# A GpSimd mask split in two and moved, and a fourth buffer for `u`, in a fused linear-attention and MLP kernel

## The chip, the cores and the metric

The kernel runs on one core of a Trainium2 chip. The metric is the device time of one execution in microseconds, lower is better. The profile is one execution, taken apart by the hardware profiler. Its engines are called PE (TensorE, with its weight loads as PEld), DVE (VectorE), ACT (ScalarE), POOL (GpSimd) and SP (SyncE).

## The reference

Sequence 2048, width 640, 32 heads of 20, MLP width 1728, bfloat16 inputs.

```
def A(x, wqkv, w_phi, wo):                       # linear attention
    q, k, v = (x @ wqkv) split into 3 x 32 heads of 20
    pq, pk = q @ w_phi[h], k @ w_phi[h]
    phi_q = concat(softmax(pq), softmax(-pq));  phi_k the same from pk
    kv, z = sum over s of phi_k[s] v[s]^T, sum over s of phi_k[s]
    o = (phi_q @ kv) / (phi_q @ z + 1e-6)
    return o @ wo

h   = x + A(layernorm(x), wqkv, w_phi, wo)
out = h + silu(layernorm(h) @ w1) @ w2
```

The state `kv` is 20 x 20 numbers for each head and sign, summed over the whole sequence, so no output of the attention can begin before the last key and value.

## The kernel before

The 2048 tokens lie on 128 partitions in 16 tiles of 640 columns. The whole program is a list of words, `ORDER`, written out by hand: each word names a small function `op_..`, with its tile or chunk, an engine or queue, and the PSUM banks (behind `@`). Every engine runs its own instructions in the order of that list; semaphores, found from the data, hold an instruction until what it reads is written and until the buffer it writes is free. So an instruction that waits holds back all that stands behind it on its engine, and nothing else.

The phases, which overlap:

1. *Statistics and weights.* `st.t` makes mean and variance of tile t on VectorE. `rs.a.b` makes 1/sqrt of the variance of tiles a to b-1, on GpSimd by a power (L275), with the negative mean beside it (L277 or L282 and L283); for a single tile the small constant is added on VectorE (L272), else on GpSimd (L274). `xn.t` normalises (L291 on VectorE, L296 on ScalarE). It is transposed by TensorE and copied out (`xt.t` at L302, `xc.t`), or by a DMA of SP's (`xd.t`). The key weights are folded with `w_phi` beforehand: `wt`, `wc` transpose them (L316, L166), `fk.c` multiplies (L331) and `fc.c` casts chunk c to `Wfk` on ScalarE (L168).
2. *Keys and values.* `kp.t` and `vp.t` are the projections (L364), 2 halves of 5 chunks each; `ke`, `kr`, `kn` make the softmax, the last one mostly on GpSimd (L407); `cc.t` adds to the state in PSUM (L420).
3. *The state's layout.* `mt` transposes a mask, and `km` multiplies the state with it into `KVBD`, which is block diagonal. The mask is `maskR`, [128, 5, 3, 32]: GpSimd sets it to one and clears it with two selects for the even and two for the odd of its five blocks (`op_mc`, L207 to L215). `mt` reads it (L221); nothing else does.
4. *Queries.* `qp`, `qe` project and exponentiate; `dp.t` multiplies by `KVBD` into four PSUM banks (L486); `dw.t` scales and adds the two signs on VectorE into `u` [128, 4, 8, 21] in float32 in SBUF (reciprocal L500, L501, then L507 and L510); `dr.t` takes the reciprocal of the denominator (L515); `do.t.half` writes a half of the output `o` on GpSimd or VectorE (L521), and is the last reader of `u`.
5. *Output projection and MLP.* `td.t` transposes `o` by a DMA, `op.t` projects (L548), `oa.t` adds the residual (L557), `sq`, `sr`, `hn`, `hd` normalise again, `up` and `ua` are the first MLP layer and SiLU (L627, L637, L649), `yp`, `yh` the second (L673, L686), `yo` adds and stores.

At the change the list reads, in words of GpSimd alone: `rs.0.1`, `mc`, `rs.1.2`, `rs.2.3`, `rs.8.10`, `rs.3.4`, `rs.10.12`. The tiles go through `dw` in the order 0, 1, 3, 2, 4, 6, 5, 9, 7, 8, 13, 12, 11, 15, 10, 14, and `u` has three buffers; a `u` takes whichever buffer is read out first. The pool that holds `u` is opened only after the state is closed, in the place of the first phases' tiles.

Of the kernel before, what the change touches and what calls it, by code (L numbers as in the profile page):

```python
# [9 lines left out]
ALU = mybir.AluOpType  # L10
# [8 lines left out]
F32 = mybir.dt.float32  # L19
# [5 lines left out]
ORDER = """  # L25
lx.0.1.a lk.0.1.s lp.a lx.1.2.s lk.4.5.a lk.1.2.s lk.2.3.s lk.3.4.s mk mo wm.512@7 wm.512@7 wm.512@7
wm.512@7 wm.512@7 wm.512@7 wm.512@7 wm.512@7 wm.512@7 wm.256@7 wt.0@0 st.0 rs.0.1 wm.256@2 wm.128@2 wt.4@1
ph ta mc st.1 wc.0.a wt.1@2 lx.2.4.s wc.1.v fk.0@4 wt.2@3 wc.2.v lx.8.12.s wc.4.a fc.0.a fk.4@6 fc.4.a
rs.1.2 xn.0.v fk.1@0 fc.1.a wt.3@2 wc.3.v fk.2@4 fc.2.a xt.0@3 xn.1.v xc.0.v st.2 rs.2.3 st.9 fk.3@6 fc.3.a
xn.2.v xt.1@2 st.8 xc.1.a rs.8.10 kp.0@0 ke.0 kp.1@4 lv.0.3.s ke.1 lv.3.5.s xt.2@3 xc.2.a vp.1@6 lq.1.s st.3  # L30
rs.3.4 st.10 vc.1.a xn.3.v xn.8.a vp.0@0 vc.0.a vp.2@4 vc.2.a xt.3@2 xc.3.a xn.9.v st.11 rs.10.12 xn.11.a
lx.4.8.s kp.2@6 st.7 ke.2 vp.3@0 lx.12.16.s kp.3@4 ke.3 xd.9 kp.9@2 st.6 xd.8 vp.8@6 xn.10.v rs.6.8 vc.3.a
xd.10 xn.6.a lq.4.s st.4 st.5 rs.4.6 xn.4.a ke.9 xn.5.a kr.0 kr.1 kn.0.p vp.9@4 vc.9.a kp.8@0 kn.1.p xd.11
vc.8.a st.13 xn.7.a kr.9 kn.9.p kp.10@2 ke.10 st.12 rs.12.14 kr.3 kn.3.p ke.8 vp.10@4 vc.10.a xd.6 kr.8
kn.8.p vp.6@6 vc.6.a kr.2 lq.3.s xn.13.a vp.11@2 vc.11.a xd.4 vp.4@0 vc.4.a kp.4@4 lq.2.s gk.2@6 st.15 xd.5
gk.1@2 kp.5@0 st.14 xd.7 ke.4 kr.4 gc.2.a xn.12.a kp.6@4 cc.3 gc.1.a ke.5 cc.0 ke.6 cc.8 cc.9 rs.14.16
xn.14.a mt kr.5 cc.1 kn.2.q lq.0.s xd.13 kp.13@2 ke.13 kr.13 l1.0.s l1.1.s vp.5@0 vc.5.a xn.15.v kr.10 xd.12
kn.5.p kn.13.q vp.13@4 vc.13.a xd.14 kp.12@2 ke.12 kr.12 kn.10.p kp.11@0 ke.11 kr.6 vp.7@4 vc.7.a gk.4@2
vp.12@0 kn.4.q l2.0.2.s l2.2.4.s gc.4.a gk.3@4 gc.3.a kp.14@2 vp.14@4 vc.14.a kn.12.p cc.2 cc.5 kr.11 ke.14
# [28 lines left out]
def kernel(  # L68
# [11 lines left out]
    nc = tc.nc  # L80

    P = nc.NUM_PARTITIONS
    T = 16
    D = 640
    C = 5
    H = 32
    DH = 20
# [11 lines left out]
    H0 = [(32 * r) // DH for r in range(C)]  # L99
# [48 lines left out]
    maskR = first.tile([P, C, 3, 32], BF16, name="maskR")  # L148
# [23 lines left out]
    def wk2():  # L172
        return late["work"]
# [29 lines left out]
        for vp in Vps:  # L203
            nc.gpsimd.memset(vp[:, :, DH : DH + 1], 1.0)

    def op_mc():
        nc.gpsimd.memset(maskR[:], 1.0)  # L207
        for r0 in range(2):
            m = maskR[:, r0::2, :, :]
            n, b0 = (C + 1 - r0) // 2, 32 * r0 - DH * H0[r0]  # L210
            nc.gpsimd.affine_select(
                out=m, in_=m, compare_op=ALU.is_ge, fill=0.0,
                base=b0, pattern=[[64 - 3 * DH, n], [-DH, 3], [1, 32]], channel_multiplier=0,
            )
            nc.gpsimd.affine_select(  # L215
                out=m, in_=m, compare_op=ALU.is_gt, fill=0.0,
                base=DH - b0, pattern=[[3 * DH - 64, n], [DH, 3], [-1, 32]], channel_multiplier=0,
            )

    def op_mt():  # L220
        nc.vector.transpose(  # L221
# [274 lines left out]
    def op_dw(t, how="p"):  # L496
        A = tl["dp", t]
        first = A[0][:, :, :, 0:21]
        w = sm.tile([P, 4, 8], F32, name="w")
        nc.vector.reciprocal(w[:], A[1][:, :, :, 21])  # L500
        nc.vector.tensor_tensor(w[:], w[:], A[0][:, :, :, 21], op=ALU.mult)  # L501
        if how == "c":
            kept = wk2().tile([P, 4, 8, 21], F32, name="kept", bufs=1)
            nc.scalar.copy(kept[:], first)
            first = kept[:]
        u = wk2().tile([P, 4, 8, 21], F32, name="u", bufs=3)
        nc.vector.tensor_tensor(  # L507
            u[:], A[1][:, :, :, 0:21], w[:].unsqueeze(3).to_broadcast([P, 4, 8, 21]), op=ALU.mult,
        )
        nc.vector.tensor_tensor(u[:], u[:], first, op=ALU.add)  # L510
        tl["u", t] = u[:].rearrange("p (a k) h c -> p a (k h) c", a=2)
# [228 lines left out]
```

## Time and profile before

| | |
|---|---|
| three runs | 239.09, 239.43, 240.14 us; median 239.43 |
| the profiled execution | 238.86 us, of which the span of the trace is 237.2 |
| granted TensorE clock | 1.00 |
| TensorE busy | 229.9 us, 97% |
| VectorE, ScalarE, GpSimd busy | 133.7, 114.9 and 92.9 us |
| DMA, mean over the span | 87 GB/s |

A row of the timeline or of a group has the start and the duration in us (the groups a mean in ns), engine, line and operation, the tiles written and read, shapes and count, and in brackets the idle time of the engine ahead of it with what ended it. Ends of matmuls are modelled, and rows that follow each other closely may overlap by some hundredths of a us. The chain of waits follows the last instruction back, at each step to what released it.

### The profile page before, as it was taken

What the parts mean: (1) busy time and instruction counts of PE and PEld (TensorE: products, weight loads), DVE (VectorE), ACT (ScalarE), POOL (GpSimd) and SP (SyncE); (2) the same over time, 40 slices, a digit from 0 to 9 for tenths busy, and PEclk for the clock granted to TensorE, in tenths of its full rate; (3) what the DMA queues carried; (4) which work ended last, traced back from release to release, by engine and by line L of the source; (5) the groups of instructions that cost most, each with busy time, mean ns of one, the idle gap of its engine ahead of it and who ended that gap; (6) DMA issues with size and microseconds to landing.
All of it is one profiled execution on the core that took longest, in us unless ns stands there. A gap on an engine that the chain in (4) does not pass through costs nothing.

```text
span 237.2 us, 6320 instructions
## 1 busy us (share of the span) xinstructions
PE 229.9 (97%) x2672; PEld 147.6 (62%) x2672; DVE 133.7 (56%) x257; ACT 114.9 (48%) x172; POOL 92.9 (39%) x184
## 2 busy tenths in 40 slices
PE   6899999999999999999999999999999999999995
PEld 2677777777544555886754645556654657688762
DVE  3899999899838989988878504321203000220032
ACT  3788998866866575664054254654014240013000
POOL 7656897798923454188071600534000100000000
PEclk9999999999999999999999999999999999999999
DMA  7964768495001849123734411103211100020012
GB/s 209 305 239 92 128 118 184 120 249 175 3 6 31 179 80 197 37 53 62 113 83 86 83 30 28 29 12 75 72 41 55 28 28 3 28 83 3 0 60 83
DMA packets 44845, 20.68 MB, mean 87 GB/s; under 512 B 34448, under 2 KB 44304, under 8 KB 44816
## 3 DMA queue, kind: packets, MB, share of 16 engines
q1 hardware_dynamic: 43728, 19.88, 36.1%
q10 hardware_dynamic: 1088, 0.39, 0.7%
q8 instruction: 21, 0.34, 0.6%
q14 instruction: 8, 0.07, 0.1%
HBM read 9.61 MB, written 2.62 MB: 52 GB/s over the span
## 4 chain that ended last, share of the span: by engine, by line
PE 88%; DVE 4%; POOL 4%; ACT 1%; DMA 1%; issue 1%; DVEq 0%; POOLq 0%
PE mm L673 24%; PE mm L627 23%; PE mm L364 18%; PE mm L548 8%; PE mm L451 7%; PE mm L486 3%; PE mm L420 2%; ACT EqT L461 1%; DMA X<-in_A_x_dram 1%; PE mm L686 1%; DVE u L507 1%; DVE u L510 1%; PE mm L637 1%; POOL RS L275 1%; PE mm L331 1%
## 5 line engine op out<-in xcount | busy, mean ns | idle before, releaser
L627 PE MATMUL mm<-HnT,w 128*128 128x512 bf16 (+1 forms) x325 | 59.1, 337 | 0.0
L649 ACT ACTIVATE shT<-mm 128x1024 bf16<-128x1024 f32 (+2 forms) x29 | 27.7, 963 | 64.3 <-PE mm L627 48.8
L673 PE MATMUL mm<-w,shT 128*128 128x320 bf16 (+2 forms) x416 | 58.5, 299 | 0.0
L673 PEld LDWEIGHTS <-shT 128*128 128x128 bf16 x416 | 39.7, 98 | 17.7 <-issue 0.8
L627 PEld LDWEIGHTS <-w 128*128 128x128 bf16 x325 | 31.3, 98 | 22.8 <-issue 0.3
L694 DVE TENSOR_TENSOR ob<-mm,X 128x640 bf16<-128x640 f32 x15 | 12.0, 817 | 47.0 <-PE mm L673 29.3
L364 PEld LDWEIGHTS <-XnT 128*128 128x128 bf16 x320 | 30.7, 98 | 11.8 <-issue 0.2
L407 POOL TENSOR_TENSOR Ek<-Ek,Sk 128x1280 bf16<-128x1280 bf16 (+2 forms) x16 | 34.6, 2184 | 3.1 <-DVE Sk L400 2.2
L557 DVE SCALAR_TENSOR_TENSOR X<-mm,X 128x640 bf16<-128x640 f32 x16 | 13.1, 823 | 21.5 <-PE mm L548 21.3
L397 DVE TENSOR_REDUCE Sk<-Ek 128x64 f32<-128x1280 bf16 x16 | 23.3, 1456 | 1.6 <-ACT Ek L389 1.6
L548 PE MATMUL mm<-wo,ot 128*128 128x320 bf16 x160 | 23.9, 299 | 0.2 <-ACT EqT L461 0.2
L521 POOL TENSOR_TENSOR o<-u,rd 128x320 bf16<-128x320 f32 x20 | 14.7, 752 | 22.7 <-DVE rd L515 14.4
L364 PE MATMUL mm<-Wfk,XnT 128*128 128x320 bf16 x160 | 23.4, 299 | 0.0
L451 PE MATMUL mm<-XnT,Wfq 128*128 128x512 bf16 x100 | 23.3, 380 | 0.0
L461 ACT ACTIVATE EqT<-mm 128x1024 bf16<-128x1024 f32 (+1 forms) x24 | 19.6, 884 | 7.4 <-PE mm L451 7.4
L364 PE MATMUL mm<-wv,XnT 128*128 128x320 bf16 x160 | 23.2, 299 | 0.0
L389 ACT ACTIVATE Ek<-mm 128x640 bf16<-128x640 f32 x32 | 20.6, 710 | 3.2 <-PE mm L364 2.7
L548 PEld LDWEIGHTS <-ot 128*128 128x128 bf16 x160 | 15.4, 98 | 7.4 <-issue 0.7
L565 ACT ACTIVATE sq<-X 128x640 bf16<-128x640 bf16 x16 | 11.7, 730 | 9.3 <-DVE X L557 7.7
L267 DVE BATCH_NORM_STATS2 stats<-X 128x6 f32<-128x320 bf16 x32 | 13.7, 468 | 3.8 <-DMA X<-in_A_x_dram 3.8
L577 POOL TENSOR_SCALAR hm<-hst,hm 128x1 f32<-128x1 f32 x16 | 4.6, 290 | 28.0 <-ACT sq L565 27.0
L451 PEld LDWEIGHTS <-Wfq 128*128 128x128 bf16 x100 | 9.1, 98 | 9.9
(78 smaller groups left out, 214.0 us busy)
## 6 DMA issues: line engine op xcount, KB each, us to landing
out_dram<-ob SPq DMA_DIRECT2D x15, 160.0 KB, 1.8
w<-in_B_w_dram SPq DMA_DIRECT2D x6, 360.0 KB, 5.2
X<-in_A_x_dram SPq DMA_DIRECT2D x3, 640.0 KB, 6.6
w<-in_B_w_dram SPq DMA_DIRECT2D x5, 320.0 KB, 4.9
wk<-in_A_wqkv_dram SPq DMA_DIRECT2D x4, 160.0 KB, 4.2
wv<-in_A_wqkv_dram SPq DMA_DIRECT2D x1, 480.0 KB, 7.3
wo<-in_A_wo_dram SPq DMA_DIRECT2D x1, 480.0 KB
w<-in_B_w_dram SPq DMA_DIRECT2D x1, 480.0 KB, 4.0
```

Source lines behind the costliest of these rows:

```text
L267: nc.vector.bn_stats(stats[:, k, :], X[:, t, k * 320 : (k + 1) * 320])
L364: nc.tensor.matmul(ps[:, half, 0:320], tok(XnT[t // GT], t)[:, c, :], W[:, c, half * 320 : (half + 1) * 320], start=(c == 0), stop=(c == C ...
L389: nc.scalar.activation(Ek[:, s, :].rearrange("p (a n) -> p a n", a=2), tl["kp", t][:, :, 0:320], AF.Exp, scale=1.0 - 2.0 * s,)
L397: nc.vector.tensor_reduce(Sk[:], tl["ek", t][:].rearrange("p s (h f) -> p (s h) f", f=DH), axis=AX.X, op=ALU.add,)
L407: nc.gpsimd.tensor_tensor(Ek3[:, 0:n], Ek3[:, 0:n], Sk[:, 0:n].unsqueeze(2).to_broadcast([P, n, DH]), op=ALU.mult,)
L451: nc.tensor.matmul(ps[:, k, :], Wfq[:, c, r * P : (r + 1) * P], XnT[g][:, c, :], start=(c == 0), stop=(c == C - 1),)
L461: nc.scalar.activation(E[:, s, rs[0] : rs[-1] + 1, :], tl["qp", g, i][:, 0 : len(rs), :], AF.Exp, scale=1.0 - 2.0 * s,)
L521: (nc.vector if eng == "v" else nc.gpsimd).tensor_tensor(tl["o", t][:, a * 320 : (a + 1) * 320].rearrange("p (h f) -> p h f", f=DH), tl["u ...
L548: nc.tensor.matmul(ps[:, half, 0:320], tl["ot", t][:, c, :], wo[:, c, half * 320 : (half + 1) * 320], start=(c == 0), stop=(c == C - 1),)
L627: nc.tensor.matmul(ps[:, i * W : (i + 1) * W], w1[:, c, fc * P : (fc + 1) * P], HnT[g][:, c, 0:W], start=(c == 0), stop=(c == C - 1), skip ...
L649: nc.scalar.activation(sh[:, a:b], tl["up", g, k][:, 0 : b - a], AF.Silu)
L673: nc.tensor.matmul(ps, shT[g][:, fc * W + i * P : fc * W + (i + 1) * P], w2[:, fc, a:b], start=first and fc == 0, stop=last and fc == FC - ...
```

## The change

`op_mc` takes an argument. `mc.0` sets the whole mask to one and does the two selects of the even blocks; `mc.1` does the two of the odd ones. `mc.0` now stands behind `rs.2.3` and `mc.1` behind `rs.3.4`, so GpSimd's order is `rs.0.1`, `rs.1.2`, `rs.2.3`, `mc.0`, `rs.8.10`, `rs.3.4`, `mc.1`, `rs.10.12`. The same five instructions are issued. The tile `u` gets four buffers for three. No other instruction changes place on any engine; in the built program the only waits that differ besides are those for a buffer of `u`, and one of an `hn` that had been covered by such a wait.

```
 ORDER
-ph ta mc st.1 wc.0.a ...
+ph ta st.1 wc.0.a ...
-... xc.0.v st.2 rs.2.3 st.9 fk.3@6 fc.3.a
+... xc.0.v st.2 rs.2.3 mc.0 st.9 fk.3@6 fc.3.a
-... st.3 rs.3.4 st.10 vc.1.a ...
+... st.3 rs.3.4 mc.1 st.10 vc.1.a ...

-    def op_mc():
-        nc.gpsimd.memset(maskR[:], 1.0)
-        for r0 in range(2):
-            m = maskR[:, r0::2, :, :]
+    def op_mc(r0):
+        if r0 == 0:
+            nc.gpsimd.memset(maskR[:], 1.0)
+        m = maskR[:, r0::2, :, :]
             (the two selects as before)

-        u = wk2().tile([P, 4, 8, 21], F32, name="u", bufs=3)
+        u = wk2().tile([P, 4, 8, 21], F32, name="u", bufs=4)
```

More of the change, by code (lines that the diff above doesn't have):

```diff
@@ L27 @@
 wm.512@7 wm.512@7 wm.512@7 wm.512@7 wm.512@7 wm.512@7 wm.256@7 wt.0@0 st.0 rs.0.1 wm.256@2 wm.128@2 wt.4@1
-ph ta mc st.1 wc.0.a wt.1@2 lx.2.4.s wc.1.v fk.0@4 wt.2@3 wc.2.v lx.8.12.s wc.4.a fc.0.a fk.4@6 fc.4.a
-rs.1.2 xn.0.v fk.1@0 fc.1.a wt.3@2 wc.3.v fk.2@4 fc.2.a xt.0@3 xn.1.v xc.0.v st.2 rs.2.3 st.9 fk.3@6 fc.3.a
+ph ta st.1 wc.0.a wt.1@2 lx.2.4.s wc.1.v fk.0@4 wt.2@3 wc.2.v lx.8.12.s wc.4.a fc.0.a fk.4@6 fc.4.a rs.1.2
+xn.0.v fk.1@0 fc.1.a wt.3@2 wc.3.v fk.2@4 fc.2.a xt.0@3 xn.1.v xc.0.v st.2 rs.2.3 mc.0 st.9 fk.3@6 fc.3.a
 xn.2.v xt.1@2 st.8 xc.1.a rs.8.10 kp.0@0 ke.0 kp.1@4 lv.0.3.s ke.1 lv.3.5.s xt.2@3 xc.2.a vp.1@6 lq.1.s st.3
[L31 to L36, printed above, removed]
+rs.3.4 mc.1 st.10 vc.1.a xn.3.v xn.8.a vp.0@0 vc.0.a vp.2@4 vc.2.a xt.3@2 xc.3.a xn.9.v st.11 rs.10.12
+xn.11.a lx.4.8.s kp.2@6 st.7 ke.2 vp.3@0 lx.12.16.s kp.3@4 ke.3 xd.9 kp.9@2 st.6 xd.8 vp.8@6 xn.10.v rs.6.8
+vc.3.a xd.10 xn.6.a lq.4.s st.4 st.5 rs.4.6 xn.4.a ke.9 xn.5.a kr.0 kr.1 kn.0.p vp.9@4 vc.9.a kp.8@0 kn.1.p
+xd.11 vc.8.a st.13 xn.7.a kr.9 kn.9.p kp.10@2 ke.10 st.12 rs.12.14 kr.3 kn.3.p ke.8 vp.10@4 vc.10.a xd.6
+kr.8 kn.8.p vp.6@6 vc.6.a kr.2 lq.3.s xn.13.a vp.11@2 vc.11.a xd.4 vp.4@0 vc.4.a kp.4@4 lq.2.s gk.2@6 st.15
+xd.5 gk.1@2 kp.5@0 st.14 xd.7 ke.4 kr.4 gc.2.a xn.12.a kp.6@4 cc.3 gc.1.a ke.5 cc.0 ke.6 cc.8 cc.9 rs.14.16
 xn.14.a mt kr.5 cc.1 kn.2.q lq.0.s xd.13 kp.13@2 ke.13 kr.13 l1.0.s l1.1.s vp.5@0 vc.5.a xn.15.v kr.10 xd.12
@@ L204, in op_mo @@
             nc.gpsimd.memset(vp[:, :, DH : DH + 1], 1.0)
-    def op_mc():
-        nc.gpsimd.memset(maskR[:], 1.0)
-        for r0 in range(2):
-            m = maskR[:, r0::2, :, :]
[L210 to L218, printed above, removed]
+    def op_mc(r0):
+        if r0 == 0:
+            nc.gpsimd.memset(maskR[:], 1.0)
+        m = maskR[:, r0::2, :, :]
+        n, b0 = (C + 1 - r0) // 2, 32 * r0 - DH * H0[r0]
+        nc.gpsimd.affine_select(
+            out=m, in_=m, compare_op=ALU.is_ge, fill=0.0,
+            base=b0, pattern=[[64 - 3 * DH, n], [-DH, 3], [1, 32]], channel_multiplier=0,
+        )
+        nc.gpsimd.affine_select(
+            out=m, in_=m, compare_op=ALU.is_gt, fill=0.0,
+            base=DH - b0, pattern=[[3 * DH - 64, n], [DH, 3], [-1, 32]], channel_multiplier=0,
+        )
     def op_mt():
```

## The prediction

> **What bounds the kernel now.** I read the page's busy table first, then the busy time by stretches, cut at the two places where the chain of waits leaves TensorE for long.
>
> ```profile
> span 237.2 us, 6320 instructions
> PE 229.9 (97%) x2672; PEld 147.6 (62%) x2672; DVE 133.7 (56%) x257; ACT 114.9 (48%) x172; POOL 92.9 (39%) x184
> ```
>
> ```profile
> 10.25:69.73 59.48, 59.48 (x953) 41.68 (x954) 53.24 (x93) 48.07 (x78) 44.70 (x46) 1.00 0.60 137
> 69.73:125.15 55.42, 53.82 (x842) 33.78 (x840) 48.38 (x102) 30.06 (x45) 25.86 (x64) 1.00 0.46 92
> 125.15:234.40 109.25, 109.20 (x807) 67.45 (x806) 26.22 (x49) 31.08 (x43) 13.93 (x43) 1.00 0.17 42
> ```
>
> The rows of the stretches give the stretch, its length, then busy time of PE, PEld, DVE, ACT, POOL, the granted clock, and DMA. TensorE works 59.48 of 59.48 us in the first of them and 109.20 of 109.25 in the last, at clock 1.00. So no edit to another engine gains anything inside those two, and a gain made ahead of one of them is carried to the end unless some wait inside it lacks slack. In the stretch between, TensorE is idle for 1.60 us, in exchanges with VectorE and ScalarE that start from TensorE's own work and so move with it. What can be won is idle time of TensorE: 237.2 less 229.9, 7.3 us, 2.8 of it behind its last matmul at 234.40. The list of waits says who waited for whom (total, times, longest), and the timeline has the wait at the head of the first full stretch.
>
> ```profile
> PE mm L486 <- DVE u L510: 1.4, 4, 0.5
> DVE u L507 <- POOL o L521: 1.3, 1, 1.3
> ```
>
> ```profile
> 10.25 0.45 PE L302 MATMUL mm<-ident,xn 128*128 128x128 bf16 x5 [0.61 <-DVE xn L291]
> ```
>
> Two waits lie under the change: the 0.61 us before the transposes of tile 1 (L302), which waited for `xn`, and one of the four waits of L486 for `u`. The row between them is VectorE's own wait for a `u` buffer, once, 1.3 us. The chain shows why `xn` came late:
>
> ```profile
> 6.78 0.44 POOL maskR L207
> ...
> 9.20 0.52 POOL RS L275
> 9.72 0.03 issue
> 9.75 0.46 DVE xn L291
> ```
>
> The mask is built from 6.78 to 9.20 us, in front of the power of `rs.1.2` (tile 1), for which `xn.1` and then TensorE wait.
>
> **The mask, first gain.** What `mc` leaves behind, on VectorE, TensorE and ScalarE (start, duration):
>
> ```profile
> 8.02 0.14 DVE L272 TENSOR_SCALAR RS<-MV 128x1 f32<-128x1 f32 x1
> 8.08 0.44 DVE L291 TENSOR_SCALAR xn<-X,MV,RS 128x640 bf16<-128x640 bf16 x1
> 8.60 0.49 DVE L166 COPY wTk<-mm 128x640 bf16<-128x640 bf16 x1
> 9.75 0.45 DVE L291 TENSOR_SCALAR xn<-X,MV,RS 128x640 bf16<-128x640 bf16 x1 [0.66 <-POOL RS L275]
> 10.11 0.48 DVE L166 COPY XnT<-mm 128x640 bf16<-128x640 bf16 x1
> 9.15 0.49 PE L331 MATMUL mm<-phb,wTk 128*128 128x140 bf16 x6
> 10.65 2.89 PE L364 MATMUL mm<-Wfk,XnT 128*128 128x320 bf16 x20
> 7.33 3.16 ACT L168 CAST Wfk<-mm 128x640 bf16<-128x640 f32 x5
> ```
>
> With the mask gone, GpSimd is free when VectorE's variance of tile 1 is done, at 8.02 + 0.14 = 8.16. The power takes 0.52, so it is there at about 8.8, and VectorE is busy with the copy of `wTk` until 9.09. Hence `xn.1` starts at 9.09 and VectorE's whole idle 0.66 us goes. The copy to `XnT` that follows (`xc.0`) ends at 10.59 now and at 9.93 then. TensorE's `kp.0` starts at 10.65, 0.06 behind that copy, and could start at 9.99; the transposes in between (`xt.1`) no longer wait, since `fk.3` ends at 9.64.
>
> What is late next: the key projection adds five chunks, and chunk 3 needs the fourth row block of `Wfk`, which ScalarE casts last of five. That row ends at 7.33 + 3.16 = 10.49 and does not move, because the casts run back to back. A matmul of that row takes 2.89 / 20, about 0.14, so chunk 3 would be due at 9.99 + 0.41 = 10.40 and can start at about 10.54; now it starts at 10.65 + 0.41 = 11.06. **The first gain is 0.52 us**, between 0 (should a further wait stand at the same place) and 0.66 (should the cast not hold it).
>
> **Where the mask goes.** `mc.0` is a memset and two selects behind `rs.2.3`, `mc.1` two selects behind `rs.3.4`. GpSimd's rows there:
>
> ```profile
> 6.71 0.50 POOL L207 MEMSET maskR<- 128x480 bf16 x1
> 8.28 0.47 POOL L211 TENSOR_SCALAR_AFFINE_SELECT maskR<-maskR 128x192 bf16<-128x192 bf16 x1
> 8.82 0.38 POOL L215 TENSOR_SCALAR_AFFINE_SELECT maskR<-maskR 128x192 bf16<-128x192 bf16 x1
> 9.17 0.54 POOL L275 TENSOR_TENSOR RS<-RS,nhalf 128x1 f32<-128x1 f32 x1
> 14.29 0.24 POOL L274 TENSOR_SCALAR RS<-MV 128x2 f32<-128x2 f32 x1 [1.47 <-DVE MV L268]
> 18.36 0.22 POOL L274 TENSOR_SCALAR RS<-MV 128x2 f32<-128x2 f32 x1 [1.43 <-DVE MV L268]
> ```
>
> From start to start `mc.0` costs 8.28 - 6.71 = 1.57 us and `mc.1` 9.17 - 8.28 = 0.89. The pauses are 1.47 and 1.43. VectorE's stream runs 0.66 ahead, so both pauses move and keep their lengths; `mc.0` overruns its own by 0.10. Queued behind it are `rs.8.10`, then the power of `rs.3.4`, for which VectorE's `xn.3` waits, and behind that TensorE's `xt.3`:
>
> ```profile
> 16.44 0.80 DVE L291 TENSOR_SCALAR xn<-X,MV,RS 128x640 bf16<-128x640 bf16 x2
> 17.73 0.44 PE L302 MATMUL mm<-ident,xn 128*128 128x128 bf16 x5
> ```
>
> Those `xn` come 0.66 - 0.10 = 0.56 earlier, TensorE only 0.52, and 17.73 - 17.24 = 0.49 us of slack lie between them already. So the mask costs nothing in its new places; without that cover it would cost the 0.10. `mc.1` has 0.54 to spare, and its reader, the transpose of the mask, comes near 40 us. No DMA is moved past anything.
>
> **The fourth `u`, second gain.** The late rows:
>
> ```profile
> 103.69 0.73 POOL L521 TENSOR_TENSOR o<-u,rd 128x320 bf16<-128x320 f32 x1
> 109.69 0.86 DVE L507 TENSOR_TENSOR u<-mm,w 128x672 f32<-128x672 f32 x1
> 110.84 1.54 POOL L521 TENSOR_TENSOR o<-u,rd 128x320 bf16<-128x320 f32 x2
> 121.90 0.19 DVE L501 TENSOR_TENSOR w<-w,mm 128x32 f32<-128x32 f32 x1
> 122.59 0.73 POOL L521 TENSOR_TENSOR o<-u,rd 128x320 bf16<-128x320 f32 x1
> 123.35 0.86 DVE L507 TENSOR_TENSOR u<-mm,w 128x672 f32<-128x672 f32 x1 [1.27 <-POOL o L521]
> 124.24 0.85 DVE L510 TENSOR_TENSOR u<-u,mm 128x672 f32<-128x672 f32 x1
> 123.89 0.74 PE L637 MATMUL mm<-HnT,w 128*64 128x256 bf16 x10
> 125.15 0.46 PE L486 MATMUL mm<-KVBD,EqT 32*128 32x44 bf16 x40 [0.52 <-DVE u L510]
> ```
>
> At 123.35 `u` of tile 15 takes the buffer that tile 12 leaves, and GpSimd reads that one last at 122.59 to 123.32. With four, the built program lets it take the buffer of tile 7, read out in the row at 110.84. It then starts at about 122.1, 1.27 us earlier, and the PSUM banks that TensorE's L486 (`dp.10`) waits for are free at 123.8 in place of 125.09. TensorE's matmul before it ends at 124.63, so the wait of 0.52 goes whole, and what is late next is TensorE itself. A follower starts about 0.05 before the modelled end of the one ahead (10.25 + 0.45 against 10.65), so **the second gain is 0.52 to 0.57; I take 0.57**. The rest of VectorE's 1.27 buys nothing, for the stretch behind has 0.05 us of idle on TensorE. The one new wait, of tile 12's `u` at 109.69 on GpSimd's row at 103.69, was over 5 us before. The other waits for `u` that go, or move to an earlier reader, cost nothing now: the list has one such wait. The other three waits of L486 are the plain sequence of matmul, two `u` steps and matmul on the same banks, and stay.
>
> **The sum.** 0.52 + 0.57 = 1.09 us off the span of 237.2. The profiled run took 238.86, 1.66 us around its span, and would take 237.8. The median of the three runs is 239.43, 0.57 above it; carried over, 1.1 us give **238.3**, 0.46% less. A measurement of this kernel can tell about 0.5%, 1.2 us, from no change.
>
> **Rivals.** *One gain only.* A wait with little slack takes one of the two back. Against it: the two full stretches, and the 0.49 us at `xt.3`, the tightest place under the mask. It gives 239.43 - 0.52, 238.9. Chance 0.10.
>
> *Nothing happens.* The mask or the buffer was put down to the wrong wait; both rows name the releaser, and the built order shows the moves, so 0.05, at 239.4.
>
> *Slower: `mc.0` stretches in its new place.* It would run beside VectorE's statistics and `xn.2`. For `xt.3` to cost TensorE anything, `mc.0` must take over the 0.49 of slack and the 0.60 by which it would let `rs.8.10` start early; each us beyond is lost. With the second gain kept, the kernel is slower by 1.2 us when `mc.0` takes 1.09 + 0.57 + 1.2 = 2.9 us more than its 1.57, nearly three times as long; at three times (3.1 more) the kernel would take about 240.9. The rows at 8.28 and 8.82 speak against it: the first ran beside the `xn` at 8.08 and took 0.47, the second has the same shape and took 0.38, so a collision costs some 0.09, and one for each of the three instructions, 0.27, stays inside the 0.49. The Trainium skill, "GPSIMD Engine Reference", Key points, has the rule that speaks against this change: GpSimd shares its SBUF interfaces with VectorE and contends with VectorE's instructions in a two-port mode or with two SBUF inputs; it gives no figure, and by it the sum could lie anywhere down to this rival's. The trace agrees in sign, with that 0.09 us. Chance 0.07.
>
> **How the numbers follow.** Both gains arrive with 0.78, one with 0.10, none with 0.05, the slower case with 0.07. In the first case the gain lies between 0.52 + 0.52 = 1.04 and 0.66 + 0.57 = 1.23 by the bounds, and three runs of one kernel spread over 239.09 to 240.14, so 1.2 us is nearly a coin's toss. What was counted at nothing (VectorE 1.27 us ahead behind 122, fewer semaphore waits) can only add, so I give that side a little more: 0.48 over 0.5%, 0.30 within. Within gets the next two cases as well, 0.45. The range runs from the upper bound (238.2) less the 0.34 by which the lowest run lies below the median, with 0.15 for what was counted at nothing, 237.7, to the one-gain case plus about as much, 239.2.
>
> **What would show it.** In the new trace TensorE's wait at L302 for `xn` is gone, `kp.0` starts near 10.0 with a short stop inside it before 10.54, GpSimd's mask rows begin near 14.29 - 1.47 - 0.66 = 12.2 and 18.36 - 1.43 - 0.66 = 16.3, TensorE's second stretch is still full, and L486 near 124.0 has no wait while VectorE's for GpSimd's `o` is gone. Wrong it would be if `mc.0` took well over 1.6 us, if `xt.3` waited, or if TensorE showed a new wait behind 126 us.

## The result, and the profile after

The changed kernel takes 238.37 us (median of 10 runs, 237.92 to 238.61), beside 239.08 for the kernel before on the same chip (10 runs): a ratio of 0.9964, 95% interval 0.9951 to 0.9976. (The ratios are not the quotients of the medians, which lie 0.71 us or 0.30% apart here.) By the ratio that is 0.36% less, inside the 0.5% that was set as the bound of what a measurement tells from no change, though the interval lies wholly below 1. The forecast was 238.3 and 0.46% less. The profiled execution's span is 236.4 us, 0.8 less than before, at a granted clock of 1.00.

The page's busy table, and the busy time by stretches, cut at the same matmuls as before (stretch, length, then PE, PEld, DVE, ACT, POOL, clock, DMA share, GB/s):

```profile
span 236.4 us, 6319 instructions
PE 230.5 (97%) x2672; PEld 147.5 (62%) x2672; DVE 134.1 (57%) x257; ACT 115.1 (49%) x172; POOL 93.0 (39%) x184
```

```profile
9.34:69.29 59.95, 59.93 (x956) 41.62 (x954) 53.35 (x93) 48.77 (x79) 47.14 (x51) 1.00 0.61 141
124.12:233.38 109.26, 109.20 (x809) 67.44 (x807) 25.71 (x48) 31.56 (x43) 13.66 (x43) 1.00 0.18 43
```

TensorE is as full as it was, in both. But the first stretch is 59.95 us long for the same work that took 59.48: it got 0.47 longer, and since ends of matmuls are modelled, the row calls the difference busy. Only the starts of the matmuls tell where it went. The waits (total, times, longest) and TensorE's timeline at the head:

```profile
PE mm L486 <- DVE u L510: 0.8, 3, 0.4
```

```profile
8.99 0.49 PE L331 MATMUL mm<-phb,wTk 128*128 128x140 bf16 x6
9.34 0.45 PE L302 MATMUL mm<-ident,xn 128*128 128x128 bf16 x5
9.74 2.98 PE L364 MATMUL mm<-Wfk,XnT 128*128 128x320 bf16 x20
12.72 0.45 PE L302 MATMUL mm<-ident,xn 128*128 128x128 bf16 x5
13.01 4.28 PE L364 MATMUL mm<-wv,XnT 128*128 128x320 bf16 x30
17.13 0.44 PE L302 MATMUL mm<-ident,xn 128*128 128x128 bf16 x5
```

L486 waits three times for `u`, no longer four. At 9.34 `xt.1` has no bracket any more. `kp.0` lasts 2.98 for 2.89 and `vp` 4.28 where other runs show 4.24: inside them are short stops.

VectorE, ScalarE and GpSimd there, then the late place on VectorE and TensorE:

```profile
8.44 0.49 DVE L166 COPY wTk<-mm 128x640 bf16<-128x640 bf16 x1
8.85 0.44 DVE L291 TENSOR_SCALAR xn<-X,MV,RS 128x640 bf16<-128x640 bf16 x1
11.22 0.89 DVE L267 BATCH_NORM_STATS2 stats<-X 128x6 f32<-128x320 bf16 x2 [0.32 <-DMA X<-in_A_x_dram]
12.27 0.39 DVE L291 TENSOR_SCALAR xn<-X,MV,RS 128x640 bf16<-128x640 bf16 x1
6.97 3.24 ACT L168 CAST Wfk<-mm 128x640 bf16<-128x640 f32 x5
```

```profile
8.11 0.67 POOL L275 TENSOR_TENSOR RS<-RS,nhalf 128x1 f32<-128x1 f32 x1 [1.17 <-DVE RS L272]
11.84 0.50 POOL L208 MEMSET maskR<- 128x480 bf16 x1
12.41 0.60 POOL L211 TENSOR_SCALAR_AFFINE_SELECT maskR<-maskR 128x288 bf16<-128x288 bf16 x1
13.08 0.49 POOL L215 TENSOR_SCALAR_AFFINE_SELECT maskR<-maskR 128x288 bf16<-128x288 bf16 x1
13.80 0.24 POOL L274 TENSOR_SCALAR RS<-MV 128x2 f32<-128x2 f32 x1 [0.23 <-DVE MV L268]
16.39 0.61 POOL L211 TENSOR_SCALAR_AFFINE_SELECT maskR<-maskR 128x192 bf16<-128x192 bf16 x1
17.07 0.38 POOL L215 TENSOR_SCALAR_AFFINE_SELECT maskR<-maskR 128x192 bf16<-128x192 bf16 x1
17.87 0.23 POOL L274 TENSOR_SCALAR RS<-MV 128x2 f32<-128x2 f32 x1 [0.42 <-DVE MV L268]
```

```profile
121.75 0.86 DVE L507 TENSOR_TENSOR u<-mm,w 128x672 f32<-128x672 f32 x1
122.64 0.85 DVE L510 TENSOR_TENSOR u<-u,mm 128x672 f32<-128x672 f32 x1
123.45 0.74 PE L637 MATMUL mm<-HnT,w 128*64 128x256 bf16 x10
124.12 0.47 PE L486 MATMUL mm<-KVBD,EqT 32*128 32x44 bf16 x40
```

GpSimd's power of tile 1 follows VectorE's variance, `xn.1` follows the copy of `wTk`, the two parts of the mask stand in pauses that still end in a wait for VectorE (0.23 and 0.42 us), and `u` of tile 15 and `dp.10` have no wait.

Start by start against before, TensorE stands as follows:

```
at (after)   shift    change  what
  7.63       -0.18            the first weights landed earlier: not the edit's doing
  9.34       -0.91    -0.73   xt.1 without its wait
 10.26       -0.81    +0.10   chunk 3 of kp.0 behind ScalarE's last cast
 12.72       -0.65    +0.16   xt.2 behind xn.2, which stood behind a statistic whose x landed late
 13.47       -0.60    +0.06   values behind the second part of wv, landed at 13.42
 43.10       -0.44    +0.18   a stop for which the profile names no releaser
124.12       -1.03    -0.59   dp.10 without its wait
233.33       -1.03            TensorE's end; the last stores end 0.3 later behind it, so the span gains 0.8
```

Without the 0.18 that the earlier landing of the weights gave, TensorE's end gained 0.85 in this profile.

### The profile page after: what moved, and what is told of

Same layout as the page of the kernel before. It is cut to its first block, busy times and chain, and to the rows that moved or that the text cites. A ratio compares the mean times of both kernels' runs of the same rounds, so it can differ in the third digit from the quotient of the medians.

```text
span 236.4 us, 6319 instructions
## 1 busy us (share of the span) xinstructions
PE 230.5 (97%) x2672; PEld 147.5 (62%) x2672; DVE 134.1 (57%) x257; ACT 115.1 (49%) x172; POOL 93.0 (39%) x184
## 4 chain that ended last, share of the span: by engine, by line
PE 92%; DVE 2%; DMA 2%; ACT 1%; issue 0%; ACTq 0%; DVEq 0%
PE mm L627 24%; PE mm L673 24%; PE mm L364 19%; PE mm L548 9%; PE mm L451 7%; PE mm L486 3%; PE mm L420 2%; DMA wk<-in_A_wqkv_dram 2%; PE mm L331 2%; ACT EqT L461 1%; PE mm L637 1%; PE mm L686 1%; DVE u L507 1%; DVE u L510 1%; PE mm L302 1%; PE mm L316 1%
## 5 line engine op out<-in xcount | busy, mean ns | idle before, releaser
L565 ACT ACTIVATE sq<-X 128x640 bf16<-128x640 bf16 x16 | 11.7, 731 | 9.3 <-DVE X L557 7.7
```

## The experiments

Each was run beside the kernel before on the same chip; ratios are to that kernel, times are medians. The kernel before measured 239.25 beside the first four, 239.21 beside the next six, and 239.16 beside the last two.

**The changed kernel again.**

> The changed kernel as it is, beside its parts on the same chip. Theory of the prediction (two waits of TensorE removed, carried to the end): 0.7 to 1.1 us less than the kernel before; TensorE's last matmul ends about 1.0 us earlier, 0.4 to 0.6 of it won before 70 us and 0.59 at 124 us. Rival (landings of the first loads and stops of TensorE without a wait decide, and differ from run to run): the shift before 70 us differs from the first profile's -0.44 by 0.2 or more, while the 0.59 stays.

238.09 us, ratio 0.9958 (0.9944 to 0.9971): 1.16 us less, a little over the range that was expected. TensorE ends 1.04 ahead of the kernel before, 0.45 of it won before 70 us and 0.59 at 124, as the theory had it.

**The mask alone.**

```
-        u = wk2().tile([P, 4, 8, 21], F32, name="u", bufs=4)
+        u = wk2().tile([P, 4, 8, 21], F32, name="u", bufs=3)
```

> The mask moved in two parts, u with three buffers. Theory: the first gain alone, TensorE ahead by 0.4 to 0.6 us from 20 us to 120 us, the 1.27 us wait of VectorE for GpSimd's o and TensorE's 0.52 us at L486 near 124 us are there again, the time 0.4 to 0.6 us under the kernel before. Rival (the gain in front is taken back later, and only the buffer counts): no difference from before at the end, though the transposes of tile 1 start early.

238.67 us, 0.9977 (0.9966 to 0.9987): 0.58 less. The waits for `u` are back:

```profile
DVE u L507 <- POOL o L521: 1.2, 1, 1.2
PE mm L486 <- DVE u L510: 1.3, 4, 0.5
```

The median is as expected, the profile is not: TensorE ends only 0.15 ahead of the kernel before. The key weights landed late in it, and TensorE's first matmul on them started at 6.71 for 6.24. Counted from there, the gain is 0.62.

**The fourth `u` alone.**

```
+ph ta mc st.1 wc.0.a ...        (the mask in its old place, in one piece)
-... rs.2.3 mc.0 st.9 ...
+... rs.2.3 st.9 ...
-... rs.3.4 mc.1 st.10 ...
+... rs.3.4 st.10 ...
```

> The fourth u alone, the mask as before. Theory: TensorE unchanged up to 124 us with its 0.61 us wait at L302 near 10 us, then 0.59 us ahead to the end, so 0.5 to 0.6 us under the kernel before; with the mask alone this adds up to the whole change within 0.3. Rival (the wait for u hides another, which then takes its place): under 0.2 us won, with a new wait of TensorE behind 125 us.

238.82 us, 0.9984 (0.9974 to 0.9994): 0.43 less. TensorE's timeline has the early wait, not the late one, and near 43 us a stop that the kernel before did not have:

```profile
10.40 0.45 PE L302 MATMUL mm<-ident,xn 128*128 128x128 bf16 x5 [0.61 <-DVE xn L291]
44.10 1.53 PE L364 MATMUL mm<-wv,XnT 128*128 128x320 bf16 x10 [0.28 <-issue]
125.22 0.47 PE L486 MATMUL mm<-KVBD,EqT 32*128 32x44 bf16 x40
```

So in this profile, where the key weights also came 0.16 later than before, TensorE ends 0.08 behind the kernel before, although `dp.10` gained its 0.59; the 0.43 is the median of twelve runs, a little under what was expected.

The two parts give 0.58 + 0.43 = 1.01 us, both together 1.16: within the intervals they add up, and each is worth about half, as the sum had it.

**The whole mask in one pause.**

```
-... rs.2.3 mc.0 st.9 ...      -... rs.3.4 mc.1 st.10 ...
+... rs.2.3 mc.0 mc.1 st.9 ...  +... rs.3.4 st.10 ...
```

> Both parts of the mask behind rs.2.3, in the first pause; four u. Theory: the mask then takes about 2.5 us where the pause has 1.5 to 1.7, so rs.8.10 and rs.3.4 come about 0.7 to 0.9 us later than in the changed kernel; the transposes of tile 3 had 0.6 us of slack there, so TensorE loses 0.1 to 0.3 us and the time lies 0.1 to 0.3 above the changed kernel. Rival (the second pause is not needed, some other cover hides it all): no difference from the changed kernel, and no wait of TensorE at L302 near 17 us. Other rival (GpSimd's selects run much slower there): more than 0.6 us lost.

238.39 us, 0.9969 (0.9959 to 0.9979): 0.30 more than the changed kernel beside it, with intervals that overlap. The timeline of GpSimd and VectorE:

```profile
14.26 0.24 POOL L274 TENSOR_SCALAR RS<-MV 128x2 f32<-128x2 f32 x1
16.41 0.80 DVE L291 TENSOR_SCALAR xn<-X,MV,RS 128x640 bf16<-128x640 bf16 x2 [0.70 <-POOL RS L275]
```

The mask now takes the pause whole (2.40 us, from 11.78), and VectorE waits 0.70 us for the power behind it. TensorE's `xt.3` loses only 0.03: the slack there swallows the rest. But start by start against the changed kernel, TensorE stops 0.09 at 18.64, 0.11 at 35.69 and 0.11 at 39.23, places that the expectation did not name and for which the profile names no releaser. Whether the later mask is behind them is not shown.

**A first part three times as long.**

```
-        nc.gpsimd.affine_select(...)              (the two selects)
+        for _ in range(4 if r0 == 0 else 1):
+            nc.gpsimd.affine_select(...)          (the two selects)
```

> The changed kernel with the two selects of mc.0 done four times instead of once (the same mask comes out), so that mc.0 takes 6 x 0.5 = about 3.0 to 3.3 us more. Theory of the prediction (a cover of about 0.5 us at the transposes of tile 3, beyond which each us is lost): rs.8.10 and rs.3.4 come 2.8 to 3.2 us later than in the changed kernel, of which some 0.3 is the rest of the pause; TensorE waits for xn at L302 near 17 to 19 us and the time lies 2.0 to 2.7 us above the changed kernel, 1.0 to 1.7 above the kernel before. Rival (GpSimd's mask has much more cover than counted, so the slower case could never have come): under 0.7 us above the changed kernel.

241.16 us, 1.0099 (1.0066 to 1.0133): 1.95 more than before. GpSimd, VectorE and TensorE (this kernel's line numbers are one higher):

```profile
17.25 0.24 POOL L275 TENSOR_SCALAR RS<-MV 128x2 f32<-128x2 f32 x1
19.39 0.80 DVE L292 TENSOR_SCALAR xn<-X,MV,RS 128x640 bf16<-128x640 bf16 x2 [3.19 <-POOL RS L276]
19.90 0.45 PE L303 MATMUL mm<-ident,xn 128*128 128x128 bf16 x5 [2.31 <-DVE xn L292]
```

From start to start `mc.0` takes 5.06 us here, 3.49 over the 1.57 of the forecast. `xt.3` starts 2.77 later than in the changed kernel, and TensorE was 0.30 late already, so 2.47 were lost there (the bracket counts 2.31, from a modelled end) and 1.02 absorbed. The 1.09 of the prediction was counted from the kernel before, with the first gain of 0.52 in it; against the changed kernel it is 0.57. So the slower rival's mechanism is real, but its threshold was set 0.45 too low; what it lacked was a reason for `mc.0` to grow. The time lies outside what was expected, which was 1.0 to 1.7 above the kernel before. Start by start, TensorE ends 3.14 behind the changed kernel: 0.30 from the head, 2.47 at `xt.3`, and most of the rest in stops of about 0.1 at 21.63, 38.67 and 42.22. These are the three places of the mask in one pause, and again no releaser is named.

**The three short stops.** First the statistic that waited for x, moved behind `xn.2`.

```
-... rs.2.3 mc.0 st.9 fk.3@6 fc.3.a xn.2.v xt.1@2 ...
+... rs.2.3 mc.0 fk.3@6 fc.3.a xn.2.v st.9 xt.1@2 ...
```

> The changed kernel with the statistics of tile 9 behind the normalisation of tile 2 on VectorE, so that the landing of the rows of tiles 8 to 11 no longer stands in front of xn.2. Theory (that landing took 0.16 us back from the first gain in the first profile, where VectorE waited 0.32 us for it): VectorE's wait no longer delays xn.2, TensorE has no stop at the transposes of tile 2, and the time is 0 to 0.2 us under the changed kernel. Rival (the values' weights, which landed at 13.42 us in that profile, 0.04 us ahead of their use, hold TensorE instead): the stop at tile 2 goes and a wait at the value projection near 13.4 us takes its place, no difference in time.

238.36 us, 0.9969 (0.9957 to 0.9981). The stop at `xt.2` is gone, but no gain in time can be seen.

Then `kp.0` with its chunks in another order, so that the row block cast last is used last.

```
-            for c in range(C):
+            for c in cs:                 # (0, 4, 1, 2, 3) for tile 0
```

> The changed kernel with the five chunks of kp.0 added in the order 0, 4, 1, 2, 3, in which ScalarE casts the folded weights. Theory (the last cast caps the first gain): the stop of TensorE inside kp.0, 0.10 us in the first profile and 0.21 in the second, is gone or under 0.08, and the rest of TensorE's second stretch moves forward by as much, so 0.05 to 0.2 us under the changed kernel. Rival (the stop is something else, or a next wait stands 0.1 us behind): the stop stays, or TensorE stops at tile 2 or at kp.1 instead.

238.60 us, 0.9968 (0.9956 to 0.9980). The stop inside `kp.0` is gone; near 43 us a stop of 0.43 has come up.

Both:

> The last two edits together, the fastest version that the first runs point to. Theory: both stops gone, TensorE 0.1 to 0.3 us ahead of the changed kernel from 14 us on, the time 0.1 to 0.3 under it and 0.9 to 1.4 under the kernel before. Rival (the landing of the values' weights is next): TensorE waits there, and the time is within 0.1 of the changed kernel.

238.25 us, 0.9966 (0.9953 to 0.9979). Neither stop is left, and the next one stands behind them: the values' projection lasts 4.43, and shows a gap of 0.19 until the values' weights land at 13.41.

```profile
12.85 4.43 PE L364 MATMUL mm<-wv,XnT 128*128 128x320 bf16 x30
```

So, with both edits kept, those weights are loaded ahead of x of tiles 8 to 11, and the statistics are reordered to suit:

```
-... lx.2.4.s ... lx.8.12.s ... lv.0.3.s ke.1 lv.3.5.s ...
+... lx.2.4.s ... lv.0.3.s ke.1 lv.3.5.s lx.8.12.s ...
-... mc.0 ... st.9 xt.1@2 st.8 xc.1.a rs.8.10 ... st.3 rs.3.4 mc.1 ...
+... mc.0 ... xt.1@2 st.3 rs.3.4 mc.1 xc.1.a ... st.9 xn.3.v st.8 rs.8.10 ...
```

> The later statistics and the other order of chunks together, and besides them: SP loads the values' weights ahead of x of tiles 8 to 11, and on VectorE and GpSimd the statistics and the power of tile 3 and mc.1 go ahead of those of tiles 8 and 9. Theory: after the two short stops at xt.2 and inside kp.0, the landing of the values' weights is what holds TensorE near 13.1 to 13.5 us; loaded first they land about 1 us earlier, that stop of about 0.2 us goes, and the kernel takes about 0.2 us less than with the two stops alone removed, 0.3 to 0.4 less than the changed kernel. Rival: x of tiles 8 to 11 now lands a microsecond later, the statistics of tiles 8 and 9 wait for it and hold VectorE's copies behind them, so that TensorE stops at vp or at xt.3 (17.1 us) by 0.2 to 0.6 us, and there is no gain or a loss. Third: anything won before 40 us is taken back by a stop of TensorE near 40 to 43.5 us for which the profile names no releaser, and the time stays that of the changed kernel.

238.34 us, 0.9962 (0.9949 to 0.9976): nothing gained. TensorE's timeline (line numbers three lower):

```profile
13.25 4.24 PE L361 MATMUL mm<-wv,XnT 128*128 128x320 bf16 x30
43.83 1.53 PE L361 MATMUL mm<-wv,XnT 128*128 128x320 bf16 x10 [0.18 <-issue]
```

The values no longer stop, 0.19 us better at that point than the kernel above. It was lost again at two places, 0.21 at 36 us and 0.34 at 43. That is the third theory's outcome, except that the stop at 36 us lies ahead of the place it had named.

> The changed kernel once more, beside the one above on the same chip. Every theory: about 1.0 us under the kernel before, 0.7 to 1.2 by the runs so far; the profile shows whether the stops of TensorE without a releaser near 40 and 43 us come at the same matmuls again.

238.20 us, 0.9965 (0.9952 to 0.9978). In this run x of tiles 8 to 11 landed in time, and `xt.2` did not stop at all; 0.20 us went at 43 us. TensorE was 0.70 ahead of the kernel before from there to 58 us, where the first two profiles have 0.44 and 0.45: the landings do move that figure, as the rival to the first of these runs had it.

**The stop at 43 us.** It comes at the eleventh matmul of the values after the state's block of 160 small ones, in some runs and not in others. What goes with it is a packet of 16 KB on the DMA queue of kind "instruction". Worked out from the records of packets and matmuls (us; the start of the packet is counted from the first matmul of the state's block, the step is from the 20th to the 21st matmul behind that block, 0.14 when nothing stops):

```
kernel                        start of packet   step
second of the two kernels below     1.64        0.14
first of the two kernels below      1.75        0.14
before                              1.86        0.16
changed, second profile             1.86        0.14
mask alone                          1.88        0.14
both stops removed                  1.98        0.14
changed, third profile              2.08        0.35
changed, first profile              2.15        0.32
longer first part                   2.17        0.34
values first                        2.36        0.48
chunks                              2.42        0.57
fourth u alone                      2.48        0.58
```

Where the step is 0.17 or longer, it ends 1.27 to 1.47 us behind the packet's end. This fits TensorE standing until its next instructions have come. That the queue is TensorE's is inferred: behind 141 us in the kernel before, TensorE starts 244 to 268 matmuls and weight loads from one such packet to the next, the other engines at most 17 instructions each. (Two kernels are not in the list, since they break its order: the later statistic, with the packet at 2.19 and a step of 0.17, and the mask in one pause, with 2.27 and 0.18. Their packets took 0.92 us, where those of the six with a longer stop took 1.07 to 1.11. And their 20th matmul itself stood 4.38 us behind the block's first, where most have 4.23 to 4.27, so most of the lateness had gone by before it.) The packet came when the DMA engines had worked off two loads of the first MLP weights, `l1.0` and `l1.1`, which are read only near 95 us. Two kernels take these away from there, to ScalarE's queue near 65 us, and to the end of SP's early loads:

```
-... kr.13 l1.0.s l1.1.s vp.5@0 ...
+... kr.13 vp.5@0 ...
-qe.0.0 qp.0.2@6 ...            (first kernel)
+qe.0.0 l1.0.a l1.1.a qp.0.2@6 ...
-l1.3.s qe.3.0 ...              (second kernel)
+l1.3.s l1.0.s l1.1.s qe.3.0 ...
```

> The changed kernel with the two first loads of the MLP weights (360 KB each) taken from SP's queue at 35.4 us and issued by ScalarE near 65 us instead. Theory: the stops of TensorE near 43 us without a releaser are instructions that arrive late. In all 12 traces so far the first matmul after the stop follows the end of a 16 KB instruction packet by 1.27 to 1.47 us, and that packet starts 1.86 to 2.48 us after the first matmul of the state's block near 38.5 us, just when the DMA engines have worked off these two loads. Without them the packet starts less than 1.7 us after that matmul, the stop near 43 us is gone, and the kernel takes 0.1 to 0.4 us less than the changed kernel, 237.8 to 238.1 us beside a kernel before of 239.2. Rival: the packet's time has nothing to do with the loads; it stays between 1.86 and 2.48, and so does the time. Third: ScalarE's two DMA issues (about 0.5 us each) don't fit in its 1.28 us of idle time before the state's cast and hold it, and the state's multiplication comes 0.2 to 1 us later, which costs that much.

> The same two loads, issued by SP behind its four loads of weights at 48.4 us. Near 43 us the same as above: packet early, no stop. But the DMA engines, idle from 55.4 us on in the changed kernel, now work to about 57.5. Theory: the instruction packet that starts at 55.2 to 55.6 us in the traces so far starts at 57 to 57.7, ends about 1.1 later, and its first matmul comes 1.3 to 1.45 us behind that, 59.4 to 60.2 us in place of about 59: a new stop of TensorE of 0.4 to 1.2 us near 59 to 60 us without a releaser, and the kernel takes 0.1 to 0.9 us more than the one above. Rival: instruction packets don't queue behind loads; that packet stays near 55.5, there is no stop near 59 us, and the time is that of the kernel above.

The first takes 237.98 us, 0.9946 (0.9932 to 0.9960), the second 237.72, 0.9939 (0.9926 to 0.9952). In both the packet comes early (1.75 and 1.64, the first of them just over what was expected), and the stop is gone. The third theory for the first kernel, that ScalarE's two issues hold the state by 0.2 us or more, did not come true: TensorE loses no more than 0.1 us to the changed kernel between 43 and 73 us. The DMA share by stretches, of the changed kernel and then of the second one, shows both the load taken away and the load put there:

```profile
36.00:40.60 4.60, 4.60 (x182) 3.48 (x181) 4.21 (x10) 4.19 (x9) 3.40 (x8) 1.00 0.94 200
55.40:57.50 2.10, 2.10 (x20) 1.57 (x19) 2.02 (x3) 1.30 (x2) 1.24 (x1) 1.00 0.10 28
```

```profile
36.00:40.60 4.60, 4.60 (x183) 3.48 (x182) 4.15 (x9) 4.19 (x9) 3.38 (x8) 1.00 0.24 46
55.40:57.50 2.10, 2.10 (x22) 1.60 (x20) 2.07 (x3) 1.42 (x3) 1.27 (x2) 1.00 1.09 331
```

The expected new stop near 59 us did not come: the next packet started at 56.31, 0.7 later than in the changed kernel, but while the loads still ran. So a packet can be delayed by loads but need not wait until they are done, and how the two share the engines stays open. The second kernel is the fastest here, 0.6% under the kernel before and some 0.2% under the changed one. That last step is not clear of the intervals (0.9926 to 0.9952 beside 0.9944 to 0.9971 for one of the changed kernel's measurements), and the first kernel's (0.9946 beside 0.9958 to 0.9965) still less: that the stop is gone rests on the traces, not on the times.

## Why the prediction was right, point by point

- **Both gains arrived, and the mechanism was the one named.** Each was undone alone, and each wait came back alone: 0.58 us for the mask and 0.43 for the buffer, forecast 0.52 and 0.57.
- **First gain.** `xt.1` gained 0.73 to 0.75 in all five profiles compared start by start with the kernel before, in place of the 0.66 of VectorE's idle. The stop behind the last cast, which the forecast named and put at 0.14, took back 0.10 in three of them and 0.21 in two (the second profile and the mask alone). That leaves 0.63 or 0.53, for a forecast of 0.52 and at most 0.66. In the first profile that cast ended at 10.21 in place of the 10.49 that was held fixed, since the weights had landed 0.36 earlier, which no edit did; chunk 3 still started 0.05 behind it, as forecast. What was not named is that other late things stood 0.1 to 0.5 us behind the removed wait: x of tiles 8 to 11, the values' weights, and the stop at 43 us. They took back 0.16, 0.06 and 0.18 in the first profile. The step of the prediction that failed is the claim that a gain ahead of the full stretch is carried through it: "full" was read from modelled ends, and what lands just in time was left out.
- **The mask costs nothing in its new places.** True of the changed kernel: `mc.0` starts at 11.84 and takes 1.96 to the next start with the idle 0.23 in it, so 1.73 for the 1.57; `mc.1` starts at 16.39. A select beside an `xn` lost 0.11 in `mc.0` (0.60 for 0.49) and 0.23 in `mc.1` (0.61 for 0.38), more than the 0.09 that the forecast gave a collision. The overrun of 0.10 did not come, since GpSimd waits for VectorE before `rs.8.10`: the late x had delayed VectorE too, and in the third profile, where x was in time, `xn.2` took 0.65 beside the memset and left GpSimd an idle 0.19. The cover at `xt.3` was larger than forecast. The row of 0.80 at 16.44, whose end (17.24) the forecast took, holds `xn` of tiles 3 and 9; `xt.3` needs the first, which ended at 16.89, so 0.84 us lay there and not 0.49.
- **Second gain.** 0.59 at `dp.10`, in the changed kernel and with the buffer alone (forecast 0.52 to 0.57), and nothing more behind it: TensorE is 1.03 ahead at 124 us and at its end.
- **"No DMA is moved past anything."** True of the order, but TensorE's stream, run earlier, meets landings that did not move, and that is where part of the gain was trimmed.
- **The sum.** 1.09 forecast; 0.71, 1.16 and 1.01 us by the medians of the three measurements, 0.96 on the mean. That is 0.13 short of it; the stops that were not named took 0.40, nothing and 0.20 in the three profiles. "What was counted at nothing can only add" was therefore wrong in sign, and the somewhat larger chance that it was given, 0.48 on more than 0.5%, was on the wrong side: 0.36% was measured.
- **Luck.** That 238.37 lies so near 238.3 is partly luck. The forecast set out from the median of three runs, 239.43, and ten runs gave 239.08, 0.35 lower; the gain beside these was 0.71, 0.38 less than forecast. The two errors cancel.

## What to carry to other kernels

When a wait is removed, list what lands or ends within the gain behind it, loads and the engine's own instructions included, before the gain is carried to the end; here three such things stood within half a microsecond. A busy row that is longer for the same matmuls is a row with stops in it: compare starts, not busy shares. Loads that nobody needs for 50 us may still cost, if they fill the DMA engines when an engine's instructions have to come in.

## What the runs showed of the hardware that was not expected

- TensorE stopped where its own instructions seem to have come late: behind a block of 160 small matmuls in about 1.7 us it stood up to 0.44 us over the even step of 0.14, with no releaser named, until 1.27 to 1.47 us after the end of a 16 KB instruction packet. That the packet's lateness is the cause is not shown outright; it rests on twelve traces that agree and on two kernels in which it came early and nothing stopped. In these two the loads themselves were gone from there as well, but in four others (the kernel before, the changed kernel's second profile, the mask alone, both stops removed) they ran and nothing stopped for more than 0.02 us. A late packet was not brought about on purpose.
- The first loads land at different times in different runs of the same kernel or of kernels that are equal up to there: the key weights' chunk that TensorE waits for between 5.8 and 6.7 us, x of tiles 8 to 11 between 10.2 and 11.7. So TensorE's first matmul on those weights differs by up to 0.9 us from profile to profile, more than either gain, and two profiles are best compared from the first full row on.
- VectorE's `xn` and GpSimd's instructions slow each other where they overlap, by 0.05 to 0.26 us: a select took 0.60 (changed) and 0.53 (longer first part) beside `xn.2` and 0.48 or 0.49 otherwise, the smaller one 0.61 and 0.38, and `xn.2` itself took 0.65 beside the memset (mask in one pause, changed kernel's third profile) and 0.39 beside a select. The last six selects of the longer first part took 0.48 each, with VectorE's statistics beside some of them: not every instruction of VectorE does it.
